# Second mixture of a three-layer kernel: weights split in double blocks on ScalarE and VectorE, hidden parts off GpSimd

## The chip, the core and the metric

The kernel runs on one core of a Trainium2 chip. The metric is device time in microseconds (us), the median of several executions. A core has five engines that each work through their own instructions in order: TensorE (PE in the profile, with its weight loads as PEld), VectorE (DVE), ScalarE (ACT), GpSimd (POOL) and SyncE (SP, which here only starts transfers). They wait for each other by semaphores.

## The reference, cut to what matters

Three layers follow one another: an attention layer, a mixture of 4 experts, in which every token goes through every expert, and a second mixture of 8 experts, in which each of the 1536 tokens is assigned to one expert with room for 192. The change is in the last one:

```python
N, D, E, F = (1536, 512, 8, 1024)
for e in range(E):
    mask = assigned == e
    h = np.maximum(x[mask] @ w1[e], 0.0)
    out[mask] = h @ w2[e]
```

`w1[e]` is 512x1024 and `w2[e]` 1024x512, both in fp32.

## The kernel before

**Two parts for every number.** Products are made of fp16 operands, two for each fp32 number: `hi` is the scaled number rounded to fp16, and `lo` what the rounding left. A product takes three matmuls (hi by hi, hi by lo, lo by hi). Weights have to be split on the chip, after they have been loaded in fp32 and a scale has been found for each matrix.

**A job** is one weight matrix (8 experts by 2 matrices). It comes in two halves `f` of 128 x 4 x 512 (1 MB, tile `raw`, loaded by SP, line 372). `w_norm` does the sum of squares of each half on ACT (line 402, `junk<-raw` 128x2048), a matmul into `pw` that adds over the partitions (line 408), and on DVE the scale from that sum (lines 297 to 302, `wse`, `wsr`). `w_split(k, c)` then does chunk `c` of 8; with `f, d = divmod(c, 4)` a chunk is block `d` of half `f`, 128x512. In the second mixture `act_hi` is 1: block 0 of a half gets its `hi` from ACT (line 429), blocks 1 to 3 from POOL (line 431). The `lo` part of each is one DVE instruction (line 438) that reads the fp32 block and the fp16 `hi`. It is issued one step later than its `hi` (it is kept in `s.lo`, and the next step issues it). Behind block 3 the half's buffer is free and the next load is started. Nine buffers go round.

**Experts.** `m_g1(e)` makes the hidden units of expert e: 8 steps of 12 matmuls, 192 columns each, with the weights as the stationary operand (line 1239, `pH` or `pq`). After every second step `hidden` takes a bank of 128x384 over: ACT applies the maximum (line 792, `H`), POOL rounds it to `hh` (`h_hi`, line 526), DVE makes `hl` (line 787). `m_g2(e)` makes the output (line 1259, 96 matmuls into two banks `pR`, each copied by ACT, line 1263, `yT`). `m_out` transposes it (line 1271), scales it on ACT (line 1273, `o`) and sends it out by an indirect transfer that POOL issues (line 1275). Tokens come in by `gather`, an indirect transfer of POOL (line 1208, `g<-rows`), and `gather_T`, a transposing transfer of SP (line 1217, `xg<-g`).

**Order.** The loop at the end of `build` goes over the experts and emits, in turn: scale copy and transfers for later experts, `m_g1(e + 1)` (with `m_out(e - 1)` between its steps), `m_g2(e)`. `play` runs these steps and calls `pump` at a fixed rate; each `pump` emits one step of the weight work, so that the weights of the experts to come are split between the matmul steps: the second matrix of expert e+1 during `m_g1(e + 1)`, the first of e+2 during `m_g2(e)`. `finish` emits what is left of a job before its weights are used. `s.early` sets how far ahead of the splits the sums of squares go. Each engine keeps the order in which its instructions were emitted. The weights of expert 0 and most of the first matrix of expert 1 are split before this loop, so 13 jobs and a rest are split in it.

Of the kernel before, what the change touches and what calls it, by code (L numbers as in the profile page):

```python
# [12 lines left out]
OP = mybir.AluOpType  # L13
# [252 lines left out]
class Net:  # L266
    def __init__(s, tc, q, k, v, probs, w1, w2, wg, v1, v2, out, n_global, n_local):
        s.tc, s.nc = tc, tc.nc
        s.q, s.k, s.v, s.probs = q, k, v, probs
        s.w = {1: (w1, w2), 2: (v1, v2)}  # L270
        s.wg, s.out = wg, out
        s.B, s.H, s.S, s.D = q.shape
        s.NQ = s.S // 128
        s.NB = s.B * s.NQ
        s.E1, s.DM, s.FF = w1.shape
        s.E2 = v1.shape[0]
        s.N = s.B * s.S
        s.CAP = s.N // s.E2
        s.G, s.L = n_global, n_local
        assert s.H * s.D == 512 and s.DM == 512 and s.FF == 1024 and s.E2 == 8  # L280
        assert s.S % 128 == 0 and s.N % s.E2 == 0 and s.CAP == 192
        assert 1 <= s.G and 1 <= s.L and s.G + s.L <= 129
        s.act_hi, s.hb, s.pw, s.nH, s.junk, s.early = 1, 2, None, 0, None, (2, 1, 0, 0)
        s.jobs = [((m, e), i) for m, n in ((1, s.E1), (2, s.E2)) for e in range(n) for i in range(2)]
        s.nload, s.kc, s.cst, s.limit, s.loadlimit = 0, 0, 0, 0, 0
        s.lo, s.lo_pool, s.hold = None, False, 0
        s.npump, s.when, s.wait = 0, {}, 0
        s.raws, s.WJ, s.nst, s.rawfree, s.W = {}, {}, {}, [], {}

# [125 lines left out]
    def w_split(s, k, c):  # L415

        V, A, G = s.nc.vector, s.nc.scalar, s.nc.gpsimd
        f, d = divmod(c, 4)
        J = s.WJ[k]
        if "hi" not in J:  # L420
            s.w_tiles(k)
        sc, (r, pool) = J["sc"], s.raws[k, f]
        h, l = J["parts"][f][0][:, d], J["parts"][f][1][:, d]
        pool_lo = s.lo_pool
        if pool_lo:
            A.activation(r[:, d], r[:, d], AF.Copy, scale=sc)
            A.copy(h, r[:, d])
        elif d < s.act_hi:
            A.activation(h, r[:, d], AF.Copy, scale=sc)  # L429
        else:  # L430
            G.tensor_scalar(h, r[:, d], sc, 0.0, op0=OP.mult, op1=OP.add)  # L431
        s.w_lo()

        def lo():
            if pool_lo:
                G.tensor_sub(l, r[:, d], h)
            else:
                V.scalar_tensor_tensor(l, r[:, d], sc, h, op0=OP.mult, op1=OP.subtract)  # L438
            if d == 3:
                if pool:  # L440
                    s.rawfree.append(pool)
                del s.raws[k, f]
                s.w_load()
        s.lo = lo
# [338 lines left out]

    def hidden(s, ps, hh, hl, sub=None):
        H = s.h_relu(ps)
        s.h_hi(H, hh)
        (sub or s.nc.vector).tensor_sub(hl, H, hh)  # L787

    def h_relu(s, ps, eng="A"):
# [799 lines left out]
    def build(s):  # L1589
# [8 lines left out]
        pool = lambda st, name, bufs, **kw: st.enter_context(tc.tile_pool(name=name, bufs=bufs, **kw))  # L1598
        re = dict(reuse_waits="tile")
        last = s.E1 - 1  # L1600
        with ExitStack() as top:
# [65 lines left out]
            for e, j0 in jobs:  # L1667
                hh = s.hp.tile([128, 8, 4, 128], F16, name="hh")
# [106 lines left out]
            s.rawfree += [raw2] * 4  # L1775
            s.loadlimit = len(s.jobs)
            s.pump(WAITS[3])
            s.act_hi = 1
            Ws = {0: W}
            s.play(s.m_g1(0, Ws[0]), RATES[0])  # L1780
            s.gather_scale(0)
# [48 lines left out]
```

## Time and profile before

| what | us |
|---|---|
| median of 3 runs (lowest, highest) | 925.57 (925.01, 926.1) |
| the profiled execution, its time | 928.81 |
| the profiled execution, span from first to last instruction | 927.0 |
| PE busy in the span | 765.6 (83%) |
| DVE busy | 670.6 (72%) |
| ACT busy | 504.8 (54%) |
| POOL busy | 433.2 (47%) |

The second mixture's experts stand in the last 190 us, from about 737 us on. The page gives shares of the whole span; what is said of this stage has to be read from stretches of it. Three views are used: the busy time of each engine in a stretch, the timeline (each instruction with its start, its duration, and in brackets the idle time of its engine before it and what ended that), and the chain of waits, which follows the work that ended last back through what released it. "issue" in that chain is time in which the engine waited for nothing that the profile shows.

### The profile page before, as it was taken

How to read it: one execution, taken by the hardware profiler on the slowest of the kernel's cores; microseconds unless marked ns; L12 is line 12 of the kernel's file. 1: busy time of each engine (PE TensorE's matmuls, PEld its weight loads, DVE VectorE, ACT ScalarE, POOL GpSimd, SP SyncE). 2: the span in 40 equal slices, each digit the busy share in tenths (PEclk: the TensorE clock that was granted, in tenths of full speed). 3: DMA queues.
4: the chain of work that ended last, by engine and by line, in shares of the span. 5: the costliest groups of instructions: out<-in, count | busy, mean ns of one | idle time of the engine just before them, and what ended most of it. 6: DMA issues, size and time to landing. Idle time of an engine off the chain costs nothing.

```text
span 927.0 us, 19443 instructions
## 1 busy us (share of the span) xinstructions
PE 765.6 (83%) x7539; PEld 551.5 (59%) x7539; DVE 670.6 (72%) x1717; ACT 504.8 (54%) x1030; POOL 433.2 (47%) x516
## 2 busy tenths in 40 slices
PE   0257889899699999999999898889777279877886
PEld 0246666667444444679778586654333179766886
DVE  7799999999445432346667787999678367888980
ACT  5787768884353030314445565656867458655521
POOL 2575867864214321061431424211454377866973
PEclk9977999999899999999999999899999689988899
DMA  9999999884621213160101111001523598877501
GB/s 226 214 164 200 175 203 177 156 135 78 193 91 46 91 46 68 24 98 18 24 1 24 17 20 24 13 1 47 215 81 126 150 350 202 232 223 211 103 18 52
DMA packets 196860, 105.21 MB, mean 113 GB/s; under 512 B 167584, under 2 KB 167584, under 8 KB 196768
## 3 DMA queue, kind: packets, MB, share of 16 engines
q1 hardware_dynamic: 194720, 97.63, 44.5%
q0 software_dynamic: 2048, 6.34, 3.2%
q8 instruction: 59, 0.97, 0.4%
q14 instruction: 33, 0.27, 0.1%
HBM read 63.00 MB, written 6.34 MB: 75 GB/s over the span
## 4 chain that ended last, share of the span: by engine, by line
PE 40%; DVE 30%; issue 9%; POOL 9%; DMA 7%; ACT 3%; SPq 1%; POOLq 0%; DVEq 0%; ACTq 0%
PE pH L818 16%; PE pY L829 13%; DVE w L438 5%; POOL w L431 3%; DVE C L951 3%; PE pR L818 2%; DVE t L690 2%; DMA xt<-xs 2%; DVE jk L954 2%; DMA xg<-g 2%; PE pY L996 2%; DVE w L457 1%; PE pH L1239 1%; POOL hh L526 1%; DVE vs L604 1%
## 5 line engine op out<-in xcount | busy, mean ns | idle before, releaser
L818 PE MATMUL pH<-xT,w 128*128 128x128 f16 (+2 forms) x2304 | 239.4, 264 | 10.7 <-DMA xT<-xs 9.2
L818 PEld LDWEIGHTS <-w 128*128 128x128 f16 x2592 | 209.8, 100 | 62.0 <-DMA xT<-xs 7.5
L829 PE MATMUL pY<-w,hh 128*128 128x512 f16 x544 | 162.3, 380 | 3.2 <-ACT y L524 1.2
L438 DVE SCALAR_TENSOR_TENSOR w<-raw,wsr,w 128x512 f16<-128x512 f32 x153 | 147.1, 1002 | 3.6 <-ACT w L429 1.8
L526 POOL TENSOR_SCALAR hh<-H 128x512 f16<-128x512 f32 (+1 forms) x87 | 59.2, 681 | 151.1 <-ACT H L792 140.2
L792 ACT ACTIVATE H<-pH 128x512 f32<-128x512 f32 (+1 forms) x94 | 53.1, 566 | 128.1 <-PE pH L818 76.0
L431 POOL TENSOR_SCALAR w<-raw,wsr 128x512 f16<-128x512 f32 x105 | 99.9, 963 | 18.0 <-DVE wsr L302 15.7
L829 PE MATMUL pY<-w,hl 128*128 128x512 f16 x272 | 103.4, 380 | 4.3 <-POOL hl L1367 3.1
L1239 PEld LDWEIGHTS <-w 128*128 128x128 f16 x768 | 73.1, 109 | 46.0 <-DVE w L438 25.0
L964 ACT ACTIVATE Cj<-C 128x128 bf16<-128x128 bf16 (+11 forms) x88 | 75.3, 855 | 43.7 <-DVE C L951 42.8
L787 DVE TENSOR_TENSOR hl<-H,hh 128x384 f16<-128x384 f32 (+1 forms) x56 | 40.0, 717 | 79.4 <-POOL hh L526 78.3
L1239 PE MATMUL pH<-xg,w 128*128 128x192 f16 x528 | 60.3, 278 | 32.5 <-DMA xg<-g 18.4
L829 PEld LDWEIGHTS <-hh 128*128 128x128 f16 x544 | 49.9, 98 | 52.4 <-issue 2.1
L951 DVE TENSOR_SCALAR C<-LR,Lg 128x1024 bf16<-128x1024 f32 (+7 forms) x88 | 64.1, 729 | 3.1 <-PE pw L970 1.8
L1259 PE MATMUL pR<-hh,w 128*128 128x192 f16 x512 | 66.3, 249 | 0.0
L1259 PEld LDWEIGHTS <-w 128*128 128x128 f16 x768 | 64.6, 99 | 0.2
L1259 PE MATMUL pR<-hl,w 128*128 128x192 f16 x256 | 63.7, 249 | 0.0
L996 PE MATMUL pY<-w,xT 128*128 128x512 f16 x192 | 60.8, 391 | 0.0
L402 ACT ACTIVATE w<-raw 128x2048 f16<-128x2048 f32 x18 | 34.3, 1904 | 42.8 <-PE pY L829 23.4
L699 ACT ACTIVATE t<-t,mx,ec 128x256 f32<-128x256 f32 (+1 forms) x96 | 55.2, 575 | 2.9
L836 DVE SCALAR_TENSOR_TENSOR y<-pY,pe,y 128x512 f32<-128x512 f32 x22 | 16.5, 749 | 51.6 <-PE pY L829 46.9
L829 PEld LDWEIGHTS <-hl 128*128 128x128 f16 x272 | 26.6, 98 | 39.6 <-POOL hl L1367 5.6
(283 smaller groups left out, 1564.4 us busy)
## 6 DMA issues: line engine op xcount, KB each, us to landing
raw<-in_moe_w_dram SPq DMA_DIRECT2D x46, 1024.0 KB, 6.4
rows<-xs SPq DMA_DIRECT2D x12, 260.0 KB, 3.1
xq<-in_q_dram SPq DMA_DIRECT2D x12, 256.0 KB, 4.0
xk<-in_k_dram SPq DMA_DIRECT2D x12, 256.0 KB, 4.6
xv<-in_v_dram SPq DMA_DIRECT2D x12, 256.0 KB, 5.2
qT<-qT SPq DMA_DIRECT2D x24, 128.0 KB, 3.9
y<-in_moe_w_dram SPq DMA_DIRECT2D x2, 1024.0 KB, 7.5
pt<-pp SPq DMA_TRANSPOSE x24, 4.5
```

The lines of the kernel that those rows point to most:

```text
L431: G.tensor_scalar(h, r[:, d], sc, 0.0, op0=OP.mult, op1=OP.add)
L438: V.scalar_tensor_tensor(l, r[:, d], sc, h, op0=OP.mult, op1=OP.subtract)
L526: s.nc.gpsimd.tensor_scalar(out, x, sc, 0.0, op0=OP.mult, op1=OP.add)
L699: s.nc.scalar.activation(t[:, o + hh], t[:, o + hh], AF.Exp, bias=mx[:, 1, hh:hh + 1], scale=e[:, 0:1], accum_out=s.SU[j][:, 2 * g + hh:2 ...
L792: s.nc.scalar.activation(H, ps, AF.Relu, scale=HS)
L818: nc.tensor.matmul(o[f], w[:, d, 128 * (f0 + f):128 * (f0 + f) + 128], x[:, :, c], start=(d == 0 and i == 0), stop=(d == 3 and i == 2))
L829: nc.tensor.matmul(py, l[:, f], w[:, f], start=(f == 0 and i == 0), stop=(f == 7 and i == 2))
L951: V.tensor_scalar(C[:, 8 * i:8 * i + n], x[:, :n, e], l, None, op0=OP.is_ge)
L964: s.nc.scalar.activation(x, C, AF.Copy, accum_out=s.AC[j][:, 1, e:e + 1])
L996: nc.tensor.matmul(py, a[:, f], w[:, f], start=(n == 0), stop=(n == 23))
L1239: nc.tensor.matmul(ps[0][:, f % 2], w[:, d, 128 * f:128 * f + 128], xg[:, :, c], start=(k == 0), stop=(k == 11))
L1259: nc.tensor.matmul(ps[0][:, d % 2], w[:, f, 128 * d:128 * d + 128], h[:, f], start=(k == 0), stop=(k == 23))
```

## The change

From the start of the second mixture's expert loop on (`s.wide = "AAVA"`), every job that is begun is split in blocks twice as wide. Even chunks make the `hi` part of two blocks at once (128x1024) on the engine that the string names for that quarter of the job: ACT, ACT, DVE, ACT. Odd chunks make the `lo` part of the same two blocks in one DVE instruction. The `lo` is no longer kept back; it comes with the next step of `pump`, as before. A job keeps 8 steps. POOL splits nothing any more. `hidden` takes `hh` from DVE where it took it from POOL. `act_hi` is no longer set back from 4 to 1, so the job that is under way at that point (the first matrix of expert 1) is finished with `hi` on ACT. Scales, matmuls, loads, gathers and their order stay.

```diff
@@ w_split
         sc, (r, pool) = J["sc"], s.raws[k, f]
+        if c == 0:
+            J["wide"] = s.wide
+        if J["wide"]:
+            d2 = slice(d // 2 * 2, d // 2 * 2 + 2)
+            h, l = J["parts"][f][0][:, d2], J["parts"][f][1][:, d2]
+            if d % 2 == 0:
+                s.scaled_on(J["wide"][c // 2], h, r[:, d2], sc)
+                s.w_lo()
+                return
+            V.scalar_tensor_tensor(l, r[:, d2], sc, h, op0=OP.mult, op1=OP.subtract)
+            if d == 3:
+                if pool:
+                    s.rawfree.append(pool)
+                del s.raws[k, f]
+                s.w_load()
+            return
@@ hidden
-        s.h_hi(H, hh)
+        s.h_hi(H, hh, "V" if s.wide else "G")
@@ build
-            s.act_hi = 1
+            s.wide = "AAVA"
```

ACT's queue while expert 3's hidden units are made, before, from the first bank on (`w1` is the second matrix of expert 3, `w0` the first of expert 4, `junk` a sum of squares, `H` a bank of hidden units, `o` an output block):

```order
L792 ACTIVATE H_10938<-pH_10911 128x384
L792 ACTIVATE H_10971<-pH_10944 128x384
L402 ACTIVATE junk_10100,wss_10975<-raw_10794 128x2048
L792 ACTIVATE H_11004<-pq_10977 128x384
L429 ACTIVATE w1_10924<-raw_10270,wsr_10725 128x512
L1273 ACTIVATE o_11031<-pY_11026,ysc_10296 96x512
L792 ACTIVATE H_11054<-pH_11009 128x384
L1273 ACTIVATE o_11065<-pY_11060,ysc_10296 96x512
L402 ACTIVATE junk_10100,wss_10975<-raw_10857 128x2048
L405 ACTIVATE wsb_11088<-wss_10975 128x1
L429 ACTIVATE w0_11103<-raw_10494,wsr_10873 128x512
```

The same place on ACT now:

```order
L808 ACTIVATE H_10906<-pH_10879 128x384
L540 ACTIVATE w1_10892<-raw_10218,wsr_10705 128x1024
L808 ACTIVATE H_10937<-pH_10911 128x384
L402 ACTIVATE junk_10100,wss_10941<-raw_10756 128x2048
L808 ACTIVATE H_10971<-pq_10943 128x384
L1289 ACTIVATE o_10995<-pY_10990,ysc_10290 96x512
L808 ACTIVATE H_11018<-pH_10976 128x384
L1289 ACTIVATE o_11028<-pY_11023,ysc_10290 96x512
L540 ACTIVATE w1_10892<-raw_10265,wsr_10705 128x1024
L402 ACTIVATE junk_10100,wss_10941<-raw_10815 128x2048
L405 ACTIVATE wsb_11049<-wss_10941 128x1
L540 ACTIVATE w0_11066<-raw_10331,wsr_10845 128x2x512 x2
```

Blocks of double width stand where there was a single block, and there are three for each job instead of two; the squares, the banks and the output blocks keep their order, and now stand behind longer splits.

DVE's queue at the same place, before (`hl` is the second part of a bank of hidden units, `wse` to `wboth` the scale of a later job):

```order
L1223 COPY ysc_10901<-g_10301 96x2
L787 TENSOR_TENSOR hl2_10910<-H_10938,hh2_10909 128x384
L438 SCALAR_TENSOR_TENSOR w1_10924<-raw_10218,wsr_10725,w1_10924 128x512 x2
L787 TENSOR_TENSOR hl2_10910<-H_10971,hh2_10909 128x384
L438 SCALAR_TENSOR_TENSOR w1_10924<-raw_10218,wsr_10725,w1_10924 128x512
L787 TENSOR_TENSOR hl2_10910<-H_11004,hh2_10909 128x384
L438 SCALAR_TENSOR_TENSOR w1_10924<-raw_10218,wsr_10725,w1_10924 128x512
L297 TENSOR_SCALAR wse_11035<-pw_4201 128x1
```

The same place on DVE now:

```order
L1239 COPY ysc_10869<-g_10295 96x2
L544 TENSOR_SCALAR hh2_10877<-H_10906 128x384
L803 TENSOR_TENSOR hl2_10878<-H_10906,hh2_10877 128x384
L432 SCALAR_TENSOR_TENSOR w1_10892<-raw_10218,wsr_10705,w1_10892 128x1024
L544 TENSOR_SCALAR hh2_10877<-H_10937 128x384
L803 TENSOR_TENSOR hl2_10878<-H_10937,hh2_10877 128x384
L432 SCALAR_TENSOR_TENSOR w1_10892<-raw_10218,wsr_10705,w1_10892 128x1024
L544 TENSOR_SCALAR hh2_10877<-H_10971 128x384
L803 TENSOR_TENSOR hl2_10878<-H_10971,hh2_10877 128x384
L544 TENSOR_SCALAR w1_10892<-raw_10265,wsr_10705 128x1024
L297 TENSOR_SCALAR wse_10999<-pw_4201 128x1
```

The four `hh` of an expert have moved onto DVE in front of their `hl`, one `hi` of each job has moved there too, and two `lo` parts have become one of double width.

POOL's queue from the gather issued in this expert's time on, before:

```order
L1208 DMA g_10906<-rows_68,idx_10028 96x1040 x2
L526 TENSOR_SCALAR hh2_10909<-H_10938 128x384
L431 TENSOR_SCALAR w1_10924<-raw_10218,wsr_10725 128x512 x2
L526 TENSOR_SCALAR hh2_10909<-H_10971 128x384
L431 TENSOR_SCALAR w1_10924<-raw_10218,wsr_10725 128x512
L526 TENSOR_SCALAR hh2_10909<-H_11004 128x384
L1274 MEMSET spacer_69 1x1
L1275 DMA out_0_dram<-o_11031,idx_10028 1536x512
L526 TENSOR_SCALAR hh2_10909<-H_11054 128x384
L431 TENSOR_SCALAR w1_10924<-raw_10270,wsr_10725 128x512
```

The same place on POOL now, up to the gather of the next expert:

```order
L1224 DMA g_10874<-rows_68,idx_10028 96x1040 x2
L1290 MEMSET spacer_69 1x1
L1291 DMA out_0_dram<-o_10995,idx_10028 1536x512
L1290 MEMSET spacer_69 1x1
L1291 DMA out_0_dram<-o_11028,idx_10028 1536x512
L1224 DMA g_11170<-rows_68,idx_10028 96x1040 x2
```

Only the indirect transfers and the small memory sets ahead of them are left.

## Rows read from the trace of the kernel before

**Rows 1.** Stretch: length, busy PE, PEld, DVE, ACT, POOL (count), clock, DMA share, GB/s.

```profile
826.00:851.00 25.00, 19.01 (x191) 17.43 (x190) 22.46 (x30) 16.16 (x23) 16.15 (x23) 0.86 0.75 215
```

**Rows 2.** Chain of waits in the expert loop: start us, length, what.

```profile
813.11 4.39 issue
...
818.38 3.30 DVE w L438 x5
...
899.65 0.44 PE pY L1271 x4
```

**Rows 3.** Timeline, PE and its weight loads: first of experts 2, 5 and 6.

```profile
774.39 0.82 PE L1239 MATMUL pq<-xg,w 128*128 128x192 f16 x8
...
844.78 0.29 PEld L1239 LDWEIGHTS <-w 128*128 128x128 f16 x3 [6.21 <-DVE w L438]
...
864.60 0.33 PE L1239 MATMUL pH<-xg,w 128*128 128x192 f16 x2
```

**Rows 4.** Timeline, POOL and DVE, around 811 to 822 us.

```profile
811.69 5.35 POOL L431 TENSOR_SCALAR w<-raw,wsr 128x512 f16<-128x512 f32 x8
...
811.41 6.84 DVE L438 SCALAR_TENSOR_TENSOR w<-raw,wsr,w 128x512 f16<-128x512 f32 x2
...
818.30 3.38 DVE L438 SCALAR_TENSOR_TENSOR w<-raw,wsr,w 128x512 f16<-128x512 f32 x5
```

**Rows 5.** Groups of 734 to 927 us: count, busy us, mean ns, idle before.

```profile
L438 DVE SCALAR_TENSOR_TENSOR w<-raw,wsr,w 128x512 f16<-128x512 f32 x107 | 106.9, 1044 | 3.0 <-POOL w L431 1.8 <-ACT w L429 1.2
...
L526 POOL TENSOR_SCALAR hh<-H 128x384 f16<-128x384 f32 x32 | 23.3, 728 | 16.6 <-ACT H L792 16.2
```

**Rows 6.** Lines by operation: ns min/median/max, first and last start, forms.

```profile
L524 ACT ACTIVATE kT<-kT,ratio x3: 1135/1140/1147, 32.6 to 163.7; 128x1024 f16<-128x1024 f16 x3
...
L948 DVE TENSOR_SCALAR_CACHE_REDUCE C<-LR,Lg x8: 1269/1274/1277, 585.1 to 642.5; 128x1024 bf16<-128x1024 f32 x8
...
L528 DVE TENSOR_SCALAR w<-raw,wsr x4: 476/704/1115, 16.6 to 255.8; 128x512 f16<-128x512 f32 x4
...
L787 DVE TENSOR_TENSOR hl<-H,hh x32: 543/558/1569, 744.7 to 905.9; 128x384 f16<-128x384 f32 x32
```

**Rows 7.** Timeline, ACT, in the same expert as rows 1.

```profile
828.21 0.48 ACT L792 ACTIVATE H<-pH 128x384 f32<-128x384 f32 x1
828.58 0.72 ACT L429 ACTIVATE w<-raw,wsr 128x512 f16<-128x512 f32 x1
829.30 0.68 ACT L1273 ACTIVATE o<-pY,ysc 96x512 f32<-96x512 f32 x1
...
831.31 1.90 ACT L402 ACTIVATE junk<-raw 128x2048 f16<-128x2048 f32 x1
...
833.53 0.71 ACT L429 ACTIVATE w<-raw,wsr 128x512 f16<-128x512 f32 x1
```

**Rows 8.** Timeline, ACT and POOL, at the end.

```profile
905.51 0.49 ACT L1263 ACTIVATE yT<-pR 128x384 f32<-128x384 f32 x1 [3.28 <-PE pR L1259]
909.47 0.49 ACT L1263 ACTIVATE yT<-pR 128x384 f32<-128x384 f32 x1 [3.47 <-PE pR L1259]
...
922.07 0.92 POOL L1275 DMA_INDIRECT out_dram<-o,idx  x1 [0.22 <-issue]
```

**Rows 9.** Transfers by issuing line: count, KB each, median us to landing.

```profile
raw<-in_moe_w_dram SPq DMA_DIRECT2D x46, 1024.0 KB, 6.4
```

**Rows 10.** Waits of 734 to 927 us: total, times, longest us.

```profile
ACT junk L402 <- DMA raw<-in_moe_w_dram: 5.8, 4, 3.4
```

**Rows 11.** Timelines of POOL, ACT, DVE and PE around the stop at 759 to 766 us.

```profile
755.60 1.23 POOL L1208 DMA_INDIRECT g<-rows,idx  x1 [0.89 <-DVE ysc L1223]
...
759.55 0.47 ACT L792 ACTIVATE H<-pH 128x384 f32<-128x384 f32 x1
...
761.75 1.51 DVE L787 TENSOR_TENSOR hl<-H,hh 128x384 f16<-128x384 f32 x1 [5.69 <-POOL hh L526]
...
766.00 0.18 PE L408 MATMUL pw<-wsb,ones 128*128 128x1 bf16 x1 [6.77 <-DVE wse L297]
```

More of the change, by code (lines that the diff above doesn't have):

```diff
@@ L285, in __init__ @@
         s.nload, s.kc, s.cst, s.limit, s.loadlimit = 0, 0, 0, 0, 0
-        s.lo, s.lo_pool, s.hold = None, False, 0
+        s.lo, s.lo_pool, s.hold, s.wide = None, False, 0, None
         s.npump, s.when, s.wait = 0, {}, 0
```

## Prediction
> **What bounds the kernel now.** I read the busy time by stretch first, then the chain of waits in the expert loop, then the timelines of the engines in it. All of it concerns the stage from 735 us on; before that the two kernels run the same instructions.
>
> In one expert's 25.0 us no engine is full: DVE is busy for 22.5, PE for 19.0, ACT and POOL for 16.2 each, and the DMA engines for 0.75 of the time, 18.8 us [rows 1]. The chain of waits says who sets the pace: it runs nearly all the time on DVE, with 4.39 us of "issue" between two `lo` instructions and then five of them in a row, 3.30 us [rows 2]. PE sits before them: its first weight load of expert 5 had waited 6.21 us for line 438 [rows 3]. So PE waits for weights, and DVE is what delivers them late.
>
> Why DVE is late stands in the timeline. While POOL makes eight `hi` blocks in a row, 5.35 us, two `lo` instructions of DVE take 6.84 us together; with POOL standing still, five take 3.38 us, 0.68 each [rows 4]. Over the stage the mean is 1.044 us for 107 of them [rows 5]. About 0.37 us of each, 39 us in all, is the stretch that comes with POOL's work. The 4.39 us of "issue" I read as the same thing: DVE held with its instruction already begun.
>
> The Trainium skill has the rule for this (SBUF — State Buffer, "Who interferes with whom"): a VectorE instruction with two inputs in SBUF and a GpSimd instruction that reads SBUF use one shared port pair, and the later one waits for the whole of the other. The trace agrees, 6.84 us against 1.36 for two. By this rule the stretch goes when POOL splits nothing; if it came from something else it stays, which is the third rival below.
>
> **The change part by part, for one expert (two jobs).**
>
> *POOL* loses 12 splits and 4 `hh`. What it keeps is the issue of transfers. Nothing waits for POOL's splits any more.
>
> *DVE.* The 16 `lo` become 8 of double width. No row shows this form; the nearest is 128x1024 with one fp32 input, 1.27 us [rows 6], and twice the mean of now, 2.09, is the other end. I take 1.27, since with POOL silent the undisturbed price should hold: 8 x 1.27 = 10.2. Two `hi` of 128x1024: between the 0.476 of the quickest 128x512 [rows 6] and twice that, 0.72 taken: 1.4. Four `hh` of 128x384 at no more than that 0.48: 1.9. Four `hl` at 0.543 [rows 6]: 2.2. Nine tiny instructions for scales: at most 3.5, what 16 x 1.044 [rows 5] and 4 x 0.558 [rows 6] leave of the 22.46 [rows 1]; half of it, 1.7. Sum 17.4, where DVE is busy for 22.5 now.
>
> *ACT.* Six `hi` of 128x1024 in the place of four of 128x512. A 128x1024 of the same function takes 1.14 [rows 6]; in a row, 128x512 costs 0.72 from start to start and a square of 2048 takes 1.90 [rows 7], so a third of the way between is 1.11: 6.7. Squares: two at 1.90 and two at 2.22 with the small cast behind them [rows 7]: 8.2. Four `H` and two `yT` at 0.37 [rows 7]: 2.2. Two `o` at 0.68: 1.4. Sum 18.5, where 16.2 is busy now.
>
> The Trainium skill (ScalarE: Activation LUTs, "What ACT_TABLE_LOAD costs") gives 280 ns + 0.833 ns per element and an overlap of 93 ns, which makes 1.04 for such a block in a row. By that the six come to 6.2, and the forecast would be some 2 us lower. The rows go into the sum.
>
> *PE.* A half of an expert's second product takes 3.96 us (two copies of its result, 905.51 and 909.47 [rows 8]), so 96 matmuls 7.92; the first product has as many. With two groups of transposes at 0.44 [rows 2]: 16.7.
>
> *DMA.* The same bytes: 18.8 us of busy share.
>
> *The order.* The risk is ACT's queue, where `H` of a bank now waits behind longer splits and squares, and where a square can wait for its load. I walked one expert with these prices. ACT's order does not close a loop that is longer than its own sum: after the second `yT` come the last split of the next `w0` (1.11) and its `lo` (1.27), ready about 2.8 us behind the end of PE's product, while PE has two banks, 4.0 us, to do before it needs them. `H` comes later than its bank, but three banks go round. `hh` then `hl` stand directly behind `H` on DVE, which has 1 to 2 us free in each expert. In the walk a half's buffer is freed some 10 us before the square that needs the load into it, and a load lands 6.4 us after its issue [rows 9]. So ACT and DMA are what is left, at 18.5 and 18.8 us. ACT waited 5.8 us in all for loads [rows 10], over 6 experts 1.0 each, and I leave that in: **19.5 us per expert**.
>
> *The stop at 759 to 766.* PE waits 6.77 us there, since a scale on DVE stands behind `hl`, `hl` behind `hh` on POOL (5.69), and `hh` behind four gathers that POOL issues from 755.60 on [rows 11]. With `hh` on DVE this falls away. What is late next is ACT, whose third `H` of expert 1 starts at 759.55 behind three squares; with the fourth `H` and two pairs of `hh` and `hl` at 0.48 each, DVE is at the scale by 762.1 and PE goes on at 762.2, 3.8 us earlier. The 8.39 us from there to expert 2 [rows 3, 11] I keep, its slow start too. Expert 2 begins at 770.6 in the place of 774.39.
>
> **The sum.** Four experts, 2 to 6, at 19.5 take 78.0 (now 864.60 - 774.39 = 90.2, 22.55 each [rows 3]). From expert 6 to 7 no squares are left, and DVE's 17.4 is the longest sum. From expert 7 on PE runs 16.7 and then what it does now from 909.47 to the end of the span at 927.0, 17.5 [rows 8]. 770.6 + 78.0 + 17.4 + 34.2 = 900.2, which is 26.8 us less than the span of 927.0. The profiled execution took 928.81, 3.24 over the median; I take the gain off the median: 925.57 - 26.8 = **899**.
>
> **The rivals.**
>
> *ACT and the loads get in each other's way* and an expert keeps the mean of now, 22.55: 12.2 us more, 911. For it: sums of 18.5, 18.8 and 16.7 lie close together, in queues that keep their order. Against: the present mean has 6 us waits of PE for DVE in it, which go.
>
> *No waits at all:* 18.5 per expert, and PE's slow start after the stop at 762 shorter by 1.5: 5.5 less, 893.
>
> *The stretch stays:* DVE is held by something other than POOL. Then 8 x 2.09, two `hi` at twice the median of 0.704 [rows 6], 8 x 0.73 for `hh` and `hl` (the mean of `hh` now [rows 5]) and 1.7 make 27.0 per expert, for five experts: 770.6 + 135.0 + 34.2 = 939.8, so 938. Against it are the five `lo` in 3.38 us.
>
> *Slower: squares stop ACT's queue.* All `hi` but one in four now come from ACT. A square that waits for its load holds up the splits behind it, which POOL made independently before, and these hold DVE, the freeing of buffers and so the next loads. Should each of four squares wait as long as the longest one now, 3.4 us [rows 10], an expert takes 18.5 + 13.6 = 32.1, the end comes 50 us later than forecast, 949. It decides from 26.2 us per expert on (26.8 / 4 = 6.7 above 19.5), that is 1.9 us of waiting for each square. Against: the 10 us between the freeing of a buffer and its square, where a landing takes 6.4 [rows 9].
>
> *It does nothing,* within 0.2%, if an expert takes 25.7 to 26.7 us; I see no mechanism that would stop there.
>
> **How the numbers follow.** Forecast 0.52; in each other's way 0.19; no waits 0.12; squares stop the queue 0.11; the stretch stays 0.03; nothing 0.03. Faster is the sum of the first three, 0.83, slower 0.14, the same 0.03; 0.2% is about what a measurement of this kernel can tell from no change. The forecast's own prices leave 18.5 to 21 us per expert, 895 to 905. The range takes in the first two rivals with 4 us below and 8 above, 889 to 919, and leaves out the last three, 0.17, and a little at either edge.
>
> **What would show it.** Right: `lo` of 128x1024 at 1.2 to 1.3 us with hardly a longer one; PE's stop at 759 down to some 3 us; expert 2 at about 770; 19 to 20.5 us from one expert to the next; ACT the fullest engine of the loop beside PE, over 0.85 of it, with waits of PE for line 438's successor (432) under 2 us per expert; the clock of the stretch above 0.95 where it is 0.86 [rows 1]. Wrong: `lo` well over 1.4 us (the stretch); ACT's waits for loads above 2 us per expert, or DMA busy 0.95 and more of the time with ACT idle (the loads); PE waiting for `hh` or for ACT in the middle of the first product.

## The result, and the profile after

The changed kernel takes **896.83 us** (median of 4 runs, 894.97 to 898.16) where the kernel before took 925.84 beside it: 29.0 us less. The ratio of the means is 0.967, 95% interval [0.963, 0.972]; that of the medians is 0.969, since one of the four runs before took 931.12. The forecast was 899 in a range of 889 to 919. The profiled execution took 895.84 us with a span of 894.1.

The stage of the second mixture first. Busy time by stretch, as in [rows 1]: one expert, the last stretch in which a sum of squares is left, and the whole from the first matmul of expert 2 to that of expert 7 (the columns are the start and end, the length, busy PE, PEld, DVE, ACT, POOL with counts, clock, DMA share, GB/s).

```profile
804.20:822.70 18.50, 17.19 (x205) 16.76 (x203) 15.49 (x28) 17.90 (x25) 4.27 (x6) 1.00 1.08 317
...
840.60:859.60 19.00, 17.25 (x204) 16.64 (x202) 16.48 (x29) 14.48 (x21) 2.04 (x4) 1.00 0.36 81
769.50:859.60 90.10, 85.59 (x1012) 83.63 (x1010) 75.67 (x132) 84.63 (x114) 20.34 (x29) 1.00 0.88 238
```

This expert takes 18.5 us, the longest of the four from 2 to 6, where the stretch of [rows 1] took 25.0; in the mean the four take 17.8, where they took 22.55. No engine was full there before; now ACT is busy for 17.90 of it and PE for 17.19, the DMA share is over 1, and POOL has 4.27 left. TensorE's granted clock is 1.00, its upper level of 2.4 GHz, where it was 0.86 in a stretch in which PE kept stopping for weights. Over the 90.1 us PE is busy for 95%, ACT for 94%.

The groups of instructions from 734 to 895 us (count, busy us, mean ns, idle time before them), which answer [rows 5, 6], DVE first, then ACT:

```profile
L432 DVE SCALAR_TENSOR_TENSOR w<-raw,wsr,w 128x1024 f16<-128x1024 f32 x52 | 65.2, 1278 | 6.3 <-ACT w L540 6.3
L803 DVE TENSOR_TENSOR hl<-H,hh 128x384 f16<-128x384 f32 x32 | 17.9, 561 | 1.1
L544 DVE TENSOR_SCALAR hh<-H 128x384 f16<-128x384 f32 x32 | 11.4, 357 | 26.5 <-ACT H L808 24.2 <-ACT w L540 2.2
L544 DVE TENSOR_SCALAR w<-raw,wsr 128x1024 f16<-128x1024 f32 x13 | 10.0, 770 | 0.0
L454 DVE SCALAR_TENSOR_TENSOR w<-raw,wsr,w 128x512 f16<-128x512 f32 x3 | 2.2, 747 | 0.0
...
L540 ACT ACTIVATE w<-raw,wsr 128x1024 f16<-128x1024 f32 x39 | 44.0, 1140 | 0.0
L402 ACT ACTIVATE junk<-raw 128x2048 f16<-128x2048 f32 x23 | 43.8, 1906 | 1.7 <-DMA raw<-in_moe_w_dram 1.6
```

The `lo` of double width costs 1.278 us, and the 52 of them lie between 1.272 and 1.285: none is stretched. Before, 107 of half the width took 106.9 us together, now these 52 and three single ones take 67.4. What DVE waits for now is ACT: the maximum `H` and the `hi` blocks.

The chain of waits in the loop (start us, length, what), as in [rows 2]:

```profile
783.28 2.08 ACT w L540 x2
...
798.92 1.90 ACT junk L402 x2
801.35 2.99 PE pR L1275 x36
804.35 2.12 PE pH L1255 x24
```

Where it ran on DVE's `lo`, it now runs on ACT's squares and splits and on PE itself, up to 810 us; behind that the view follows POOL's transfers back and says little of the loop. The waits from 735 to 895 us (total, times, longest) say the same; PE stands still for `lo` for 0.8 us in the whole stage, its weight loads for 1.7, and ACT 1.6 us for loads ([rows 10]: 5.8 before):

```profile
PEld L1255 <- DVE w L432: 1.7, 4, 0.8
ACT junk L402 <- DMA raw<-in_moe_w_dram: 1.6, 2, 1.1
...
PE pH L1255 <- DVE w L432: 0.8, 2, 0.5
```

The same in the kernel before, from 734 to 927 us; with the `pq` matmuls PE lost 19.5 us to `lo` there:

```profile
PEld L1239 <- DVE w L438: 25.0, 20, 6.2
...
PE pH L1239 <- DVE w L438: 13.5, 13, 5.7
...
PE pq L1239 <- DVE w L438: 6.0, 1, 6.0
```

PE's timeline (start us, length, what; in brackets the idle time before and what ended it) at the stop of [rows 11] and at the first matmuls of experts 2, 6 and 7 [rows 3]:

```profile
760.85 0.19 PE L408 MATMUL pw<-wsb,ones 128*128 128x1 bf16 x1 [2.93 <-DVE wse L297]
...
769.45 0.74 PE L1255 MATMUL pq<-xg,w 128*128 128x192 f16 x7
...
840.57 0.33 PE L1255 MATMUL pH<-xg,w 128*128 128x192 f16 x2
...
859.56 2.23 PE L1255 MATMUL pH<-xg,w 128*128 128x192 f16 x24
```

ACT's timeline at the second copy of expert 6's product, as in [rows 8]:

```profile
876.56 0.49 ACT L1279 ACTIVATE yT<-pR 128x384 f32<-128x384 f32 x1 [3.47 <-PE pR L1275]
```

The stop is 2.93 us where it was 6.77. Expert 2 begins at 769.5, expert 6 at 840.6, expert 7 at 859.6 (before, 774.4 and 864.6 for the first two).

### The profile page after: what moved, and what is told of

It reads as the page before. It is cut to its first block, busy times and chain, and to the rows that moved or that the text cites. A ratio compares the mean times of both kernels' runs of the same rounds, so it can differ in the third digit from the quotient of the medians.

```text
span 894.1 us, 19304 instructions
## 1 busy us (share of the span) xinstructions
PE 755.8 (85%) x7539; PEld 544.6 (61%) x7539; DVE 645.1 (72%) x1710; ACT 528.1 (59%) x1046; POOL 334.4 (37%) x403
## 4 chain that ended last, share of the span: by engine, by line
PE 41%; DVE 25%; issue 12%; DMA 9%; ACT 7%; POOL 4%; SPq 1%; POOLq 0%; DVEq 0%; ACTq 0%
PE pH L834 16%; PE pY L845 14%; DVE C L967 3%; PE pR L834 2%; PE pY L1012 2%; ACT junk L402 2%; DVE jk L970 2%; DMA xt<-xs 2%; DVE t L706 2%; DMA xk<-in_k_dram 2%; PE pH L1255 2%; DMA xg<-g 2%; DVE w L473 1%; PE pR L1275 1%; POOL out_dram L1291 1%
## 5 line engine op out<-in xcount | busy, mean ns | idle before, releaser
L834 PEld LDWEIGHTS <-w 128*128 128x128 f16 x2592 | 209.0, 100 | 61.8 <-DMA xT<-xs 7.1
L542 POOL TENSOR_SCALAR hh<-H 128x512 f16<-128x512 f32 x55 | 36.6, 665 | 134.3 <-ACT H L808 123.8
L1255 PEld LDWEIGHTS <-w 128*128 128x128 f16 x768 | 65.5, 100 | 23.4 <-DMA xg<-g 18.5
L432 DVE SCALAR_TENSOR_TENSOR w<-raw,wsr,w 128x1024 f16<-128x1024 f32 x52 | 65.2, 1278 | 6.3 <-ACT w L540 6.3
L1255 PE MATMUL pH<-xg,w 128*128 128x192 f16 x528 | 49.8, 254 | 20.2 <-DMA xg<-g 18.3
L803 DVE TENSOR_TENSOR hl<-H,hh 128x384 f16<-128x384 f32 (+1 forms) x56 | 34.6, 617 | 44.2 <-POOL hh L542 43.1
L1275 PEld LDWEIGHTS <-w 128*128 128x128 f16 x768 | 64.7, 99 | 2.3 <-issue 2.0
L540 ACT ACTIVATE w<-raw,wsr 128x1024 f16<-128x1024 f32 (+1 forms) x49 | 50.7, 1053 | 6.5 <-DVE wsr L302 6.5
L695 PE MATMUL pS<-kT,qT 128*128 128x128 f16 x176 | 29.4, 245 | 25.9 <-DVE mx L706 9.9
```

The source lines that it names most:

```text
L432: V.scalar_tensor_tensor(l, r[:, d2], sc, h, op0=OP.mult, op1=OP.subtract)
L540: s.nc.scalar.activation(out, x, AF.Copy, scale=sc)
L834: nc.tensor.matmul(o[f], w[:, d, 128 * (f0 + f):128 * (f0 + f) + 128], x[:, :, c], start=(d == 0 and i == 0), stop=(d == 3 and i == 2))
L1255: nc.tensor.matmul(ps[0][:, f % 2], w[:, d, 128 * f:128 * f + 128], xg[:, :, c], start=(k == 0), stop=(k == 11))
L1275: nc.tensor.matmul(ps[0][:, d % 2], w[:, f, 128 * d:128 * d + 128], h[:, f], start=(k == 0), stop=(k == 23))
```

## The experiments

The theory: DVE's two-input `lo` was stretched by the splits on POOL; with them gone DVE keeps up, and PE and ACT set the pace. The rivals: the gain comes from blocks of double width (half as many instructions), from `hh` on DVE, or from something on POOL other than its reading. Every ratio is to the kernel before on the same chip; the kernel after is 0.9674 [0.9632, 0.9715]. Its 931.12 beside it moves that ratio by more than 0.1%, so where two kernels differ by less than 1%, the stretch from the first matmul of expert 2 to that of expert 7 in their profiles is given as well: 113.4 us in the kernel before, 90.1 in the kernel after.

### One part at a time

**`hh` alone.** The kernel before, with only the middle units' first part moved to DVE from the expert loop on:

```diff
-        s.h_hi(H, hh)
+        s.h_hi(H, hh, "V" if s.wide else "G")
...
-            s.act_hi = 1
+            s.act_hi, s.wide = 1, True
```

> The kernel before with one part of the change alone: hh of the expert loop on DVE. Theory A (POOL's splits stretch DVE's lo instructions, and with them gone the stretch goes): the stop of PE at 759 us shrinks from 6.8 to about 3 us, the lo of 128x512 keep a mean of 0.95 to 1.05 us, the experts keep their 22 to 25 us, 918 to 924 us in all. Theory B (the detour of hh over POOL is what held the loop): most of the gain comes with this part, 900 to 910 us.

Measured 919.32 us, ratio 0.991 [0.989, 0.993]. Groups of DVE from 734 us on:

```profile
L438 DVE SCALAR_TENSOR_TENSOR w<-raw,wsr,w 128x512 f16<-128x512 f32 x107 | 88.9, 877 | 11.6 <-POOL w L431 11.1 <-ACT w L429 0.5
...
L413 DVE TENSOR_TENSOR wboth<-wsr 128x1 f32<-128x1 f32 x6 | 12.1, 2025 | 0.0
```

The timelines of POOL and of DVE at one place in the loop:

```profile
809.95 11.25 POOL L431 TENSOR_SCALAR w<-raw,wsr 128x512 f16<-128x512 f32 x8
...
815.03 3.39 DVE L438 SCALAR_TENSOR_TENSOR w<-raw,wsr,w 128x512 f16<-128x512 f32 x5
```

The time came as expected. The mean of `lo` did not, it fell to 0.877, and the stop of PE is 4.58 us and not some 3. The two engines still hold each other. Six `wboth`, one element per partition but with two inputs, take 12.1 us, the longest 5.2 us (in the kernel after each is 0.15). And here it is POOL that is held: its eight `hi` take 11.25 us where [rows 4] shows 5.35, while five `lo` run at their bare 3.39. Which engine pays changes from place to place; that one of them pays does not. `hh` alone is worth 0.9%.

**Splits alone.** The kernel after, with `hh` left on POOL:

```diff
-        s.h_hi(H, hh, "V" if s.wide else "G")
+        s.h_hi(H, hh)
```

> The changed kernel with hh left on POOL: the splits alone. Theory A: the lo of 128x1024 stay near 1.3 us but for those that meet one of the four hh of an expert, the experts take 18 to 19.5 us, the stop at 759 us stays at 5 to 7 us; 899 to 905 us. Theory B: 915 us or more.

Measured 898.6 us, 0.968 [0.967, 0.970]. Groups from 734 us on, two of DVE and one of POOL:

```profile
L432 DVE SCALAR_TENSOR_TENSOR w<-raw,wsr,w 128x1024 f16<-128x1024 f32 x52 | 67.0, 1312 | 8.2 <-ACT w L540 8.1
L803 DVE TENSOR_TENSOR hl<-H,hh 128x384 f16<-128x384 f32 x32 | 20.0, 629 | 33.9 <-POOL hh L542 33.5 <-POOL spacer L1290 0.4
...
L542 POOL TENSOR_SCALAR hh<-H 128x384 f16<-128x384 f32 x32 | 27.0, 849 | 40.9 <-ACT H L808 40.5
```

PE's timeline at the stop:

```profile
765.30 0.19 PE L408 MATMUL pw<-wsb,ones 128*128 128x1 bf16 x1 [5.12 <-DVE wse L297]
```

Nearly the whole gain is here, a little more than expected. The 32 `hh` left on POOL stretch `lo` a little (1.312) and `hl` more (0.629), but the loop has room for that: from expert 2 to expert 7 it takes 90.2 us, as in the kernel after. The stop is still 5.12 us, and in the profiled execution its 2.2 us do not come back; the medians are too close to tell. So the parts do not add: `hh` is worth 0.9% while POOL splits, and nothing that can be measured once it does not.

**Width alone.** Double blocks as in the kernel after, but three of four `hi` on POOL as before, and `hh` on POOL too:

```diff
-            s.wide = "AAVA"
+            s.wide = "AGGG"
...
-        s.h_hi(H, hh, "V" if s.wide else "G")
+        s.h_hi(H, hh)
```

> Double blocks, but three quarters of each job's hi on POOL and hh on POOL, as before the change: the width alone. Theory A: POOL's reads stretch the lo again, their mean is 1.6 us or more, and the time lies at 915 to 935 us, near that of the kernel before. Theory C: the width brings its gain here too, 910 us or less.

Measured 921.54 us, 0.993 [0.990, 0.996]. Groups of DVE and POOL from 734 us on:

```profile
L432 DVE SCALAR_TENSOR_TENSOR w<-raw,wsr,w 128x1024 f16<-128x1024 f32 x52 | 85.2, 1667 | 3.9 <-POOL w L542 1.9 <-ACT w L540 1.0 <-POOL spacer L1290 0.9
...
L542 POOL TENSOR_SCALAR w<-raw,wsr 128x1024 f16<-128x1024 f32 x39 | 60.5, 1561 | 2.2 <-PE pw L408 1.9
```

With POOL splitting, the same `lo` takes 1.667 instead of 1.278. Width as such is worth 0.7%. (Like all runs that start from the kernel after, this one finishes the job under way with `hi` on ACT; that small part of the change was not run alone.)

**Everything but the width.** The kernel after without its branch for double blocks; the four quarters of a job keep their engines, in blocks of 128x512:

```diff
-        if J["wide"]:
-            d2 = slice(d // 2 * 2, d // 2 * 2 + 2)
...
+        elif J["wide"]:
+            s.scaled_on(J["wide"][c // 2], h, r[:, d], sc)
```

> The changed kernel with single blocks of 128x512 in the place of double ones, on the same engines quarter by quarter, hh on DVE. Theory A: the lo take 0.74 us and are not stretched; ACT has 12 splits of 0.65 instead of 6 of 1.04 in an expert, 1.6 us more, and ACT sets the pace, so about 20 us per expert and 902 to 907 us. Theory C (the gain is that of fewer, wider instructions): more than half of it goes, 912 us or more.

Measured 901.1 us, 0.972 [0.970, 0.975], a little below what was expected. Groups of DVE:

```profile
L442 DVE SCALAR_TENSOR_TENSOR w<-raw,wsr,w 128x512 f16<-128x512 f32 x107 | 75.7, 744 | 8.4 <-ACT w L528 8.4
```

`lo` stands at its bare price, 0.744. From `hh` alone (0.991) to here the only step is POOL's 81 splits going to ACT and DVE: 1.8%. Double width on top is worth some 0.5% more, with intervals that just overlap; the profiles agree with it, 94.6 us from expert 2 to expert 7 here and 90.1 in the kernel after. It is ACT, with twice as many splits, that is busy for 90.4 of the 94.6.

### What it is on POOL: reading, writing, or its queue

Three kernels put useless work on POOL into the kernel after, behind each of the 52 double blocks. It moves none of the kernel's data.

**Three copies that read.** 128x512 from fp32 to fp16, the form of POOL's old splits:

```diff
                 s.scaled_on(J["wide"][c // 2], h, r[:, d2], sc)
+                for _ in range(3):
+                    G.tensor_scalar(s.ddst, s.dsrc, 1.0, 0.0, op0=OP.mult, op1=OP.add)
```

> The changed kernel with work added on POOL that nobody waits for: three instructions for each double block that copy one 128x512 tile from fp32 to fp16, 156 in all. Theory A (POOL's reads hold DVE): the mean of the lo rises from 1.28 us to 1.5 us or more, single ones take several us, DVE is busy for 15 us more or beyond, and the time rises to 903 to 925 us. Theory D (it was the waiting for POOL's results, not its reads): lo stay at 1.28 us and the time at 895 to 899 us.

**Three writes.** The same place and size, nothing read: `G.memset(s.dsrc, 1.0)`.

> As the kernel with added reads, but the added instructions of POOL are memory sets of 128x512 in fp32, which write and read nothing. If it is POOL's reading that holds the two-input lo of DVE: lo stay at 1.28 us, hh and the hi of DVE may be stretched a little, 895 to 900 us. If any busy POOL holds DVE: as with the reads, lo at 1.5 us or more and 903 us or more.

Reading: 946.38 us, 1.020 [1.016, 1.023]. Writing: 900.5 us, 0.970 [0.967, 0.972]. Groups of DVE and POOL from 734 us on in the reading kernel:

```profile
L434 DVE SCALAR_TENSOR_TENSOR w<-raw,wsr,w 128x1024 f16<-128x1024 f32 x52 | 72.7, 1422 | 4.1 <-ACT w L542 4.1
...
L431 POOL TENSOR_SCALAR ddst<-dsrc 128x512 f16<-128x512 f32 x156 | 135.5, 868 | 12.1
```

The same in the writing kernel:

```profile
L434 DVE SCALAR_TENSOR_TENSOR w<-raw,wsr,w 128x1024 f16<-128x1024 f32 x52 | 65.2, 1278 | 4.9 <-ACT w L542 4.9
L805 DVE TENSOR_TENSOR hl<-H,hh 128x384 f16<-128x384 f32 x32 | 17.9, 560 | 1.1
L546 DVE TENSOR_SCALAR hh<-H 128x384 f16<-128x384 f32 x32 | 15.3, 477 | 23.0 <-ACT H L810 23.0
...
L431 POOL MEMSET dsrc<- 128x512 f32 x156 | 87.6, 562 | 8.2
```

87.6 us of writing left `lo` at 1.278 and `hl` at 0.560, within a nanosecond of what they are without it; only one-input instructions got slower, `hh` from 0.357 to 0.477. From expert 2 to expert 7 this kernel takes 89.0 us, no more than the kernel after. So POOL being busy does not stretch `lo`; POOL reading does. But the reading kernel lost far more time than either theory gave it, while its `lo` rose by less. Its POOL timeline shows why:

```profile
824.90 20.43 POOL L431 TENSOR_SCALAR ddst<-dsrc 128x512 f16<-128x512 f32 x15
845.56 1.03 POOL L1226 DMA_INDIRECT g<-rows,idx  x1 [0.22 <-issue]
```

And so does a line of its waits from 820 us on (total us, times, longest):

```profile
PE pH L1257 <- DMA xg<-g: 18.2, 2, 11.4
```

POOL fell behind: 15 copies in a row stood ahead of a gather, and PE waited for the rows, up to 11.4 us. That is POOL's queue, not DVE, and this run mixes the two.

**One copy that reads** in place of three, `range(1)`, to take the queue away:

> The kernel after, with one useless GpSimd copy of 128x512 from fp32 to fp16 (SBUF to SBUF) behind each double block from the expert loop on, 52 in all instead of the 156 before, about 45 us of GpSimd instead of 135. With 156, GpSimd worked off up to 15 copies in a row (20.43 us) ahead of a gather, so their time held the gathers back as well as VectorE. With 52 the gathers should leave in time. If reads by GpSimd stretch VectorE's two-input `lo` by contending, its mean rises by a third of what 156 did or more (1.278 to 1.33 or more, with single ones near 1.6), no wait for gathered rows over 2 us appears, and the time is 897 to 906 us. If the 946 us came from contention rather than from the queue, even a third of it shows: 908 or more.

Measured 904.83 us, 0.975 [0.971, 0.980]: 0.8% over the kernel after, with intervals that just overlap; from expert 2 to expert 7 it takes 96.0 us for 90.1. Groups of DVE and POOL:

```profile
L434 DVE SCALAR_TENSOR_TENSOR w<-raw,wsr,w 128x1024 f16<-128x1024 f32 x52 | 70.4, 1377 | 6.8 <-ACT w L542 6.7
L805 DVE TENSOR_TENSOR hl<-H,hh 128x384 f16<-128x384 f32 x32 | 22.0, 688 | 1.1
...
L431 POOL TENSOR_SCALAR ddst<-dsrc 128x512 f16<-128x512 f32 x52 | 68.9, 1325 | 3.5
```

The gathers leave in time, and the stretch is still there: `lo` 1.377 (most at 1.279, a few up to 2.02), `hl` 0.688, and the copies themselves 1.325 us each, which took 0.67 in [rows 4] (eight in 5.35). What the 946 us lost beyond this came with three times the reads and with the late gathers; how much with which stays open.

### What sets the pace afterwards

**All four `hi` on ACT**, and **two of four on DVE**, in place of "AAVA":

```diff
-            s.wide = "AAVA"
+            s.wide = "AAAA"
```

> The changed kernel with all four quarters of a job's hi on ACT. If ACT sets the pace of the loop: 2.1 us more per expert over five of them, less what the last ones have in hand, 903 to 908 us, PE with 2 us of waits more per expert. If the loads or PE set it: 896 to 899 us.

> The changed kernel with two quarters of a job's hi on DVE, two on ACT. If ACT alone sets the pace: 1.5 to 2 us less per expert, until PE's 17 us and DVE's 17 us bind, 889 to 894 us. If the loads (DMA busy share 1.0 in the loop) bind as well: 895 to 899 us.

"AAAA" takes 902.23 us, 0.972 [0.970, 0.974], just under what was expected; its experts begin at 769.0, 787.3, 807.2, 827.2 and 847.2, so 20 us each once the loop runs, and DVE's `lo` waits 17.5 us for ACT's `hi` in the stage (6.3 in the kernel after). "AVVA" takes 895.81 us, 0.966 [0.964, 0.968], no different from the kernel after. So more work on ACT costs its full price, and less of it gains nothing: something else stands right behind ACT.

**Half of the loads**, with "AAVA" and with "AVVA". Loads issued from the expert loop on bring only two of their four blocks; squares and splits read these twice, so the engines' work is the same and half of the weights are not the ones asked for (of the edit, the load):

```diff
-            s.nc.sync.dma_start(r, src.rearrange("(k p) f -> p k f", p=128))
+            q = 2 if s.wide else 4
+            s.nc.sync.dma_start(r[:, 0:q], src.rearrange("(k p) f -> p k f", p=128)[:, 0:q])
```

> The kernel after, with each weight load issued from the expert loop on cut to its first two of four blocks (0.5 MB instead of 1 MB); squares and splits read these two blocks twice, so every engine does the same instructions and half of the weights isn't the one asked for. The DMA share falls from 1.0 to some 0.6. If ScalarE alone sets the pace (its sum 17.9 of 17.8 us per expert) the time stays within 0.3% of the kernel after, 894 to 899. If waits for loads set it, the squares' wait of 1.6 us goes and an expert comes down to TensorE's 17.2: 890 to 894.

> The same halved loads, and two of the four splits of a job on VectorE (AVVA). This relieves ScalarE (16.0 us per expert) and the loads at once, where AVVA alone (895.8) gained nothing that can be measured. If loads are the second bound behind ScalarE, an expert comes down to TensorE's 17.1 and the time to 889 to 893. If it stays at 894 to 898, what is left is TensorE and the order of the queues, and neither ScalarE nor the loads are worth more work.

891.84 us, 0.961 [0.959, 0.964], with "AAVA", and 893.09 us, 0.963 [0.961, 0.966], with "AVVA". Busy time from the first matmul of expert 2 to that of expert 7 (columns as above), first with "AVVA" and whole loads:

```profile
768.80:857.80 89.00, 85.48 (x1012) 83.28 (x1010) 80.17 (x139) 75.31 (x104) 21.94 (x29) 1.00 0.87 242
```

With "AAVA" and half loads:

```profile
769.40:857.80 88.40, 85.66 (x1013) 83.67 (x1011) 76.06 (x132) 84.34 (x114) 21.17 (x29) 1.00 0.62 153
```

With "AVVA" and half loads:

```profile
768.60:855.80 87.20, 84.91 (x1012) 83.33 (x1011) 81.17 (x141) 75.32 (x104) 21.72 (x29) 1.00 0.64 155
```

Against the 90.10 us of the kernel after, half loads save 1.7, "AVVA" 1.1, both 2.9, and then PE is busy for 84.91 of 87.20. With half loads and "AAVA" the experts from 3 on begin 17.9 us apart each time: the 18.5 and 19.0 of the kernel after are gone, and what is left is ACT's sum of 17.9, not PE's 17.2, which was expected if loads set the pace. In the times only the loads can be told, some 0.6%, and hardly: the intervals overlap a little. The 902 us with "AAAA" and these three say that ACT, the loads and PE lie within 3 us of each other over five experts, and that PE's own 85 us is the floor. Neither ACT nor the loads are worth much more work while PE's work stays as it is.

## Why the prediction was right, point by point

**What bounded the kernel: right, and shown.** POOL's splits stretched DVE's two-input `lo`, and PE waited for it. "Width alone" keeps the splits and loses the gain; "splits alone" has nearly all of it; writes on POOL leave `lo` alone and reads stretch it. The price taken for the undisturbed `lo`, 1.27 from a row of another operation [rows 6], was 1.278. The rival "the stretch stays" falls. The Trainium skill (SBUF — State Buffer, "Who interferes with whom") agrees, in a part that the prediction did not use too: it says that a two-input VectorE instruction contends with GpSimd's reads and not with its mere writes, as 1.377 against 1.278 shows here.

Four readings were less exact than they look. The weight load of expert 5 that waited 6.21 us is not that expert's first, whose matmuls start at 838.47. The 39 us of stretch set a recorded mean (1.044) against a distance from start to start (0.68); like against like, 1.044 and the 0.744 of "everything but the width", it is 0.30 each, and DVE's busy time in `lo` fell from 106.9 to 75.7 us, by 31. "The trace agrees" holds for the contention and not for its length: if the later instruction waits for one other, that is 0.67 us here, but one `lo` of [rows 4] is recorded at 6.18, through all eight splits, and from 811.41, before the first of them at 811.69. And the chain does not run on DVE nearly all the time: from 850 to 883 us it runs mostly on POOL's splits and `hh`. There POOL is the one held, seven splits in 8.90 us where [rows 4] has eight in 5.35, while three `lo` beside them took their bare 2.06. POOL's timeline of the kernel before:

```profile
862.00 8.90 POOL L431 TENSOR_SCALAR w<-raw,wsr 128x512 f16<-128x512 f32 x7
```

So POOL's reading and DVE's two inputs cost each other time, and the prediction priced one side of it. It made no difference to the sum, since both sides go with the splits.

**The stop: right.** 2.93 us for "some 3". PE went on at 760.85 for 762.2, but 1.3 us of that are older: the stage's first matmul starts at 738.24 where it started at 739.55. The 8.39 us kept from there to expert 2 became 8.6, and expert 2 began at 769.5 for 770.6.

**An expert: the step that was mis-sized.** 19.5 us were forecast for experts 2 to 6; 16.9, 17.9, 18.5 and 17.9 came, 17.8 in the mean (71.1 us for 78.0). The first of the four ran at PE's own pace before the change already, which the mean of 22.55 hides; priced at 19.5, it holds 2.6 of the 6.9 us. Its stretch in the kernel before (columns as in [rows 1]):

```profile
774.39:791.15 16.76, 16.76 (x204) 16.74 (x203) 12.24 (x20) 14.62 (x22) 13.70 (x17) 1.00 1.02 253
```

By the terms of the sum:

- ACT's sum of 18.5 is 17.9 in a full expert (the stretch from 804.20 to 822.70). Two blocks of 128x1024 in a row take 2.18 us on ACT, so 1.04 each from start to start where 1.11 was taken from the rows of other shapes. That is 0.4 of the 0.6. It is also the 1.04 that the Trainium skill (ScalarE: Activation LUTs, "What ACT_TABLE_LOAD costs") gives; the measured number stands by itself.
- 1.0 us of load waits per expert was kept from the kernel before. It is 1.6 in the whole stage, and 0.54 in these four experts. This was the largest miss of a term, 3.5 us over the four, and it was a wait carried over without asking which of the two kernels it belongs to.
- DVE's 17.4 is 15.1 (75.67 for five experts): `hh` 0.357 for 0.48, and the rest in `lo` standing in a row at 1.2 from start to start and tiny instructions. It cost nothing since DVE was not the longest.
- PE's 16.7 is 16.9 to 17.25; the DMA sum of 18.8 is 18.1 in the mean, 20.0 in the longest (share by length). A load did not take longer to land: from 735 us on the median is 6.2 us after its issue, where it was 6.7 before. The loads are not free either, since half of them gone gave 1.7 us back.

Here are these two rows, after and before, which answer [rows 9] for the stage alone; the columns are count, KB each and us from issue to landing:

```profile
raw<-in_moe_w_dram SPq DMA_DIRECT2D x23, 1024.0 KB, 6.2
...
raw<-in_moe_w_dram SPq DMA_DIRECT2D x23, 1024.0 KB, 6.7
```

**From expert 6 to 7: the one step that failed.** "No squares are left, and DVE's 17.4 is the longest sum." It took 19.0. ACT's timeline in this stretch still has a square, and it waits for its load:

```profile
844.40 1.91 ACT L402 ACTIVATE junk<-raw 128x2048 f16<-128x2048 f32 x1 [1.11 <-DMA raw<-in_moe_w_dram]
```

PE's timeline there, its rows with idle time: it stands still for `lo` twice, and for the sum of that square:

```profile
841.22 0.67 PE L1255 MATMUL pH<-xg,w 128*128 128x192 f16 x6 [0.32 <-DVE w L432]
...
842.41 3.47 PE L1255 MATMUL pH<-xg,w 128*128 128x192 f16 x40 [0.53 <-DVE w L432]
...
846.78 0.16 PE L408 MATMUL pw<-wsb,ones 128*128 128x1 bf16 x1 [0.90 <-ACT wsb L405]
```

These three are 1.75 us, just what 19.0 is over PE's own 17.25. With half loads this stretch takes 17.9.

**The tail: right.** 34.2 forecast; 859.56 to 894.1 is 34.5, with 17.5 from the second copy at 876.56, as before.

**The sum.** 769.5 + 71.1 + 19.0 + 34.5 = 894.1 for the forecast 770.6 + 78.0 + 17.4 + 34.2 = 900.2. Of the 6.1 us between them 6.9 are the four experts and 1.1 the earlier start; 1.9 go the other way. In the medians it is 2 us, since the gain was taken off a median that lay 3.24 us under its profiled execution; this time the profiled one lies under the median by 1.0. That closeness is luck: by the spans the gain is 32.9 us and not 26.8.

**The rivals.** "No waits at all", 18.5 per expert, was the nearest for the loop: waits there are nearly none. Its 893 lies 4 us below the result, the forecast 2 above it. "In each other's way" did not come: it held ACT and the loads for what would collide, and they do lie close, but they cost 3 us and not 12. "Squares stop ACT's queue" did not come; two squares waited 1.6 us together. Of the signs named for it, `lo` at 1.2 to 1.3, the stop, expert 2 at 770, ACT over 0.85 (it is 0.94), PE's waits under 2 us and the clock over 0.95 (it is 1.00) came; 19 to 20.5 us per expert did not. A DMA share of over 0.95 did come, which was named as a sign against it; but ACT stood busy beside it, not idle. A second sign against it came once, PE waiting for ACT in the middle of a first product, behind a square that had waited 0.54 us for its load. PE's timeline in the kernel after:

```profile
811.23 1.15 PE L1255 MATMUL pH<-xg,w 128*128 128x192 f16 x12 [0.81 <-ACT H L808]
```

## What to carry to other kernels

When two-input instructions of DVE are slower than their quickest, look at what POOL reads at that time: taking the reads away was worth more here (1.8%) than making DVE's instructions wider and fewer (0.5 to 0.7%), and parts that cure the same wait do not add up. After such a change ask again for every wait carried over into the sum whether its cause is still there, and take the distance from start to start of instructions that stand in a row, not their recorded length, on both sides of a comparison. Price each round of a loop by itself before taking a mean of them. The gain ends at the next engine, here PE at 95%: moving more work between ACT and DVE was worth nothing.

## What the runs showed of the hardware that was not expected

87.6 us of writing on POOL cost two-input instructions of DVE nothing (`lo` 1.278 and 1.278, `hl` 0.561 and 0.560), but made one-input ones from fp32 to fp16 slower, `hh` 0.357 to 0.477, `hi` 0.770 to 0.846 (ahead of that run this was named as possible). Between a reading POOL and a two-input DVE instruction either can be the one that is held, at different places in one kernel: in the kernel before eight splits of POOL took 5.35 us in [rows 4], with `lo` held, and seven took 8.90 at 862.00 us, with `lo` at its bare price. An instruction need not be large to be held: with `hh` moved, a `wboth` of one element per partition took 5.2 us. Why one engine wins at one place and the other elsewhere stays open.
